# Two stacked layers of memory attention and a gated feed-forward, one core: the order of softmax and gate work, of the memory weighting in one-layer steps, and the form of the last output block are changed

## The chip, the cores and the metric

The kernel runs on one core of one Trainium2 chip. The metric is the device time of one execution in microseconds (us); the figure quoted for a kernel is the median of its runs. Five engines work side by side and meet through semaphores: TensorE (PE in the profile, with its weight loads as PEld), VectorE (DVE), ScalarE (ACT), GpSimd (POOL) and SyncE (SP). Matmul results go to PSUM, which this kernel uses as eight banks of 512 f32 values per partition.

## The reference

The input is 2048 tokens of 448 features. Two layers follow each other. Each is an attention with a memory that is handed from segment to segment, and then a feed-forward with a gate (ReGLU), both with a layer norm in front and a residual around:

```python
# attention: 64 segments of 32 tokens, 8 memory tokens, 16 heads of 256
for s in range(n_seg):
    h = jnp.concatenate([mem, x[:, s*32:(s+1)*32, :]], axis=1)       # 40 tokens
    q, k, v = (jnp.einsum('btd,dhe->bhte', h, W) for W in (Wq, Wk, Wv))
    scores = jnp.where(mask, jnp.einsum('bhqe,bhke->bhqk', q, k) * scale, -1e9)
    o = jnp.einsum('bhqk,bhke->bhqe', softmax(scores), v)
    o = jnp.einsum('bhte,hed->btd', o, Wo)
    mem = o[:, :8, :]                                                 # to the next segment
    outs.append(o[:, 8:, :])
# feed-forward, 448 -> 1792 -> 448
h = relu(x @ W_gate) * (x @ W_up);  y = h @ W_down
# whole
x = x + attention(layernorm(x)); x = x + feed(layernorm(x))          # twice, same weights
```

The memory of a segment comes out of the segment before, so the 64 segments of a layer run one after another.

## The kernel before, in words

**Weights.** Wq and Wk are folded into one matrix per head ahead of the loop (`A_sb`), Wv and Wo into another (`B_sb`). With these a step needs, for each half of the heads: `project` (hidden rows times `A_sb`, tiles `prj`, copied to `TQ` and `TZ`), `scores`, `softmax`, a transpose of the probabilities (`flipped`, tile `pps`, copied to `PT`), their product with the hidden rows `hk` (`weigh_m` and `weigh_x`, tiles `ya`, `yb`, `y1`, `y2`, copied to `Y`), and the product of `Y` with `B_sb` (`project_out` for features 0 to 383 in tile `ox`, `project_last` for the last 64 in `o3`).

**Steps.** `step` (line 695) handles one segment of each active layer. The second layer runs `LAG` = 4 segments behind the first, so steps g = 0 to 3 and 64 to 67 have one layer, g = 4 to 63 have two, and the hidden rows of both stand side by side in one matmul (80 columns, 40 in one-layer steps). `ms` are the layers whose memory goes on, `xs` those whose previous output is projected now. The heads fall into half 0 and half 1. Each half has a softmax of the memory queries (tile `Sm`, `m0` and `m1`, probabilities `PM`) and one of the segment's own queries (`Sx`, `x0` and `x1`, `PX`). `softmax` (line 651) gives four closures, called by index: [3] `lift`, [0] `first`, [1] `exp`, [2] `second`. With a mask (both layers active) `lift` adds it and `first` takes the maximum and subtracts it; without one `lift` does both and `first` nothing. `exp` is ACT's exponential on tile `se`, `second` sums, inverts and scales to `PM` or `PX`.

**Feed-forward.** Every odd step from g = 3 on carries one `Feed` (line 469): the feed-forward of 64 tokens of each layer. At g = 3 and 5, and in the last ones, only one layer has tokens, so it is 64 columns and not 128. `residual` adds the attention's output (collected with features on the partitions in `OT`, transposed on PE) to the tokens `x` and takes the layer-norm statistics (`row_stats`: batch-norm statistics and aggregate on DVE, `rstd` on POOL at lines 251 and 252); `norm` and `xposed` make `xT`. The 14 tiles of 128 gate and up columns go in units 0 to 3 of 4, 4, 4 and 2. `products(u)` puts a unit's up products in PSUM tile `ups` and its gate products in `gps`; for u = 3 both share one bank named `gps`. `gated(u)` copies `ups` to `ut` on ACT (the "up copy", a CAST) and then makes `hh` = max(`gps`, 0) * `ut` on DVE. `down` is the product with `Wd_sb` in `dps`; `down_out` adds the residual and stores.

**Order.** PE's order is that of the program text: `in_order` (line 80) ties every matmul to the one before. DVE and ACT are wrapped in `InOrder` (line 93), which does the same there, so all their instructions carry line 102; every matmul is line 144 (`mm`), every transpose line 152 (`tr`). A wait at the head of one of these queues therefore holds all behind it.

**PSUM banks.** `bank` (line 121) gives a new tile the one of the eight banks, among those not held, that by a running estimate comes free soonest: after a tile's last matmul the bank counts as free `after` ns later, a value given by name (700 if none). The tile's first matmul then waits for the last reader of whatever tile was in that bank before. For x1 of a feed step that value is 8000, for `gps` 1600, for `ups` 1000.

**The end.** At g = 67 (`end`) both x softmaxes are interleaved with the first products of the feed before; the outputs of half 0 and 1 go to `YB` column `XL`. Then a step g = 68 that only projects out (`if not chains`), and the lines from 1018 on: the residual, the rest of the feed before (`fed`), and the last feed (`ff`), whose output leaves by two stores on SP (line 569), beside a copy `xh` of the residual that came by DMA (line 489).

Of the kernel before, what the change touches and what calls it, by code (L numbers as in the profile page):

```python
# [9 lines left out]
F32 = mybir.dt.float32  # L10
I32 = mybir.dt.int32
AF = mybir.ActivationFunctionType
ALU = mybir.AluOpType
# [47 lines left out]
def build_kernel(ctx, tc, A_x, A_mem0, A_Wq, A_Wk, A_Wv, A_Wo, B_W_gate, B_W_up, B_W_down, out,  # L61
# [407 lines left out]
    class Feed:  # L469
# [10 lines left out]
        def residual(self):  # L480
            tp = bank([P, 4, 128], BF, "otp")
            for kd in range(4):
                tr(tp[:, kd, :], OT[:, kd, :], ident[:])
            dve.tensor_tensor(self.x[:], tp[:].rearrange("p k d -> p (k d)")[:, 0:DM], self.x[:], op=ALU.add)
            self.st = row_stats(self.x)
            if not self.first:
                self.xh = main.tile([P, DM // 2], BF, tag="xh", name="xh", bufs=2)
                for c in range(2):
                    nc.sync.dma_start(self.xh[64 * c:64 * c + 64, :], self.x[0:TB, HALF[c]])
# [70 lines left out]
        def down_out(self):  # L560
            i, dps = self.i, self.dps
            if self.first:
                dve.tensor_tensor(self.nx[TB:P, :], dps[TB:P, 0:DM], self.x[TB:P, :], op=ALU.add)
                self.st = row_stats(self.nx)
                nc.sync.dma_start(xa[(i + 2) % 3][0:TB, :], self.nx[TB:P, :])
            if self.second and not self.first:
                dve.tensor_tensor(self.xh[:], dps[:, 0:DM // 2], self.xh[:], op=ALU.add)
                for c in range(2):
                    nc.sync.dma_start(out_dram[block(i - LAG // BLK), HALF[c]], self.xh[64 * c:64 * c + 64, :])
            elif self.second:  # L570
                dve.tensor_tensor(self.x[0:TB, :], dps[0:TB, 0:DM], self.x[0:TB, :], op=ALU.add)
                nc.sync.dma_start(out_dram[block(i - LAG // BLK)], self.x[0:TB, :])
            if self.first and i + 3 < nblk:
                nc.sync.dma_start(self.x[TB:P, :], x_dram[block(i + 3)])
# [76 lines left out]
    def softmax(Sp, n, dst, keep, tag, mask=None):  # L651

        mx = main.tile([P, n], F32, tag=f"mx{tag}", name="mx")
        se = main.tile([P, n, L], F32, tag=f"se{tag}", name="se")
        ssum = main.tile([P, n], F32, tag=f"ssum{tag}", name="ssum")
        rs = main.tile([P, n], F32, tag=f"rs{tag}", name="rs")

        def lift():
            if mask is not None:
                dve.tensor_tensor(se[:], Sp[:], mask, op=ALU.add)  # L660
            else:
                shift(Sp)

        def first():
            if mask is not None:
                shift(se)

        def shift(src):
            dve.tensor_reduce(mx[:], src[:], axis=AX.X, op=ALU.max)
            dve.tensor_tensor(se[:], src[:], mx[:].unsqueeze(2).to_broadcast([P, n, L]), op=ALU.subtract)  # L670

        def exp():
            act.activation(se[:], se[:], AF.Exp, scale=SCALE)

        def second():
            dve.tensor_reduce(ssum[:], se[:], axis=AX.X, op=ALU.add)
            dve.reciprocal(rs[:], ssum[:])
            if keep is not None:
                dve.tensor_tensor(rs[:], rs[:], keep, op=ALU.mult)
            dve.tensor_tensor(dst[:, :, 0:L], se[:], rs[:].unsqueeze(2).to_broadcast([P, n, L]), op=ALU.mult)  # L680

        return first, exp, second, lift
# [12 lines left out]
    def step(g, ff, pre, late):  # L695
# [7 lines left out]
        if g == 0:  # L703
            lo = 0
        end = g == nsteps - 1
        if g == nsteps:
            lo, hi = XL, XO[1] + SEG
        ox = None

        def ox_open():  # L710
# [14 lines left out]
        def scores(hf, m, x):  # L725

            if not ms:
                m = False
            both = len(chains) == 2
            Sm = bank([P, 2, L], F32, "Sm", 1100) if m else None  # L730
            Sx = bank([P, 4, L], F32, "Sx", 2500 if hf == 0 else 3500 if ff is None else 8000) if x else None
            groups = [(half, c) for half in range(2) for c in chains]

            def mem(kds):
                for kd in kds:
                    mm(Sm[:, :, :], queries(hf, 2, kd), moving(hb, j, kd, (0, 1)),
                       start=(kd == KD[0]), stop=(kd == KD[-1]), skip_group_check=True)
# [12 lines left out]
            if m and x and not both:  # L750
                mem(KD)
                mask()
                own(KD)
            elif m and x:
                mem(KD[:3])
                own(KD[:3])
                mem(KD[3:])
                own(KD[3:])
            elif m:
                mem(KD)  # L760
            elif x:
# [19 lines left out]
        def weigh_x(hf, hk, PT, between=None):  # L781

            def keep(eng, c, t0, src):
                n = src.shape[-1] // SEG
                xo = XL if end else XO[c]
# [37 lines left out]
        def project_last():  # L823
# [21 lines left out]
            if g == nsteps:  # L845
                places = [(0, XO[1]), (SEG, XL)]
            else:
                places = [(o + (TB if c == 0 else 0), XO[c]) for c in xs]
            for to, x in places:
                dve.tensor_tensor(OT[r, 3, to:to + SEG], o3[r, x:x + SEG], os[r, x:x + SEG], op=ALU.add)  # L850

        def finish():
# [5 lines left out]
            if g == nsteps:  # L858
                dve.tensor_copy(OT[:, 0:3, 0:SEG], ox[:, :, XO[1]:XO[1] + SEG])
                dve.tensor_copy(OT[:, 0:3, SEG:TB], ox[:, :, XL:XL + SEG])  # L860
                return
            for c in xs:
                o2 = o + (TB if c == 0 else 0)
                dve.tensor_copy(OT[:, 0:3, o2:o2 + SEG], ox[:, :, XO[c]:XO[c] + SEG])
# [3 lines left out]
                for u in us:  # L868
                    ff.gate_up(u)

        if not chains:
            ox_open()
            project_out(0, 0, NT)
            project_last()
            project_out(1, 0, NT)
            finish()
            return None, None

        project(0, chains, hb, j, BANKS[0][0:2], pre)
        hk = hk_make()  # L880
# [9 lines left out]
        def memory_0():  # L890
            nonlocal m0
            m0, _ = scores(0, True, False)
            m0[3]()
            m0[1]()

        if late is not None:
# [14 lines left out]
            nonlocal pm  # L911
            pm = flipped(PM[0], 1, "m0") if ms else None

        project(1, chains, hb, j, BANKS[1][4:5], pre1, True, None, flip_m0)
        if ff is not None:
            ff.xposed_out()
        _, x0 = scores(0, False, True)
        weigh_m(0, hk, pm)
        m1, x1 = scores(1, True, True)
        m1[3]()  # L920
        m1[1]()
        x0[3]()
        if end:
            x1[3]()
            ff.open_rows((0, 1))
            x0[1]()
            x1[1]()
            x0[2]()
            ff.products(0)
            px0 = flipped(PX[0], 2, "x0", act)  # L930
            ff.gated(0)
            ff.products(1)
            x1[2]()
            px1 = flipped(PX[1], 2, "x1", act)
            ff.gated(1)
            weigh_x(0, hk, px0)
            weigh_x(1, hk, px1)
            return {}, None
        if ff is not None:
            x1[3]()  # L940
# [4 lines left out]
            x0[1]()  # L945
            m1[2]()
            x0[2]()
            x1[0]()
            x1[1]()
            feed(0)  # L950
            next_piece()
            ff.products(1)
            x1[2]()
            pm = flipped(PM[1], 1, "m1", act) if ms else None
            ff.gated(1)
            ff.products(2)
            px0 = flipped(PX[0], 2, "x0", act)
            weigh_m(1, hk, pm)
            ff.gated(2)
# [45 lines left out]

    dve.on = act.on = True
    pre, late = project_early(0, active(0), hTb[0], 0), None
    for g in range(nsteps + 1):
        if g == LAG - 1:
            set_mem(LAG, mem0T[:].unsqueeze(2), (1,))  # L1010
        i = (g - 3) // 2
# [4 lines left out]
            pre, late = step(g, None, pre, late)  # L1016

    ff = Feed(nblk + LAG // BLK - 1)
    fed.open_rows((2,))
    ff.residual()  # L1020
    for u in (2, 3):
        fed.products(u)
    for u in (2, 3):
        fed.gated(u)
    fed.down_part(0, 8)
    ff.norm()
    fed.down_part(8, FT)
    ff.xposed()
# [64 lines left out]
```

## Time and profile before

| | |
|---|---|
| median of 3 runs | 1599.95 us (1599.68 to 1600.59) |
| the profiled execution: its time | 1600.88 us |
| its span (first to last instruction) | 1599.0 us |
| mean granted TensorE clock | 0.999 |
| PE busy | 1574.0 us, 98% of the span, 41160 matmuls and transposes |
| PE weight loads busy | 1450.5 us, 91% |
| DVE busy | 1124.8 us, 70%, 3704 instructions |
| ACT busy | 744.1 us, 47%, 2088 instructions |
| POOL busy | 78.2 us, 5% |
| largest groups on PE | `prj` 541.7 us (15232 matmuls, 199 ns mean), `ox` 450.4 us (11424, 200 ns) |

How to read it: a matmul's recorded length (about 0.2 us) is much longer than the time between the starts of two (some 0.03 to 0.06 us), because matmuls are pipelined. The sum of lengths is counted once where they overlap, so "busy" says that some matmul was under way, not that PE ran at its best. A line of a timeline gives start, length, engine, line, operation, output and inputs with shapes, how many instructions were put together, and in brackets the idle time before it with what ended that. In a line of the chain that ended last, shares are of the span. A row of waits gives the engine, what waited, on what, then the sum of the waits in us, how often, and the mean.

### The profile page before, as it was taken

To read this page: it belongs to the slowest core of one execution; us is meant where nothing else is said; L and a number is where in the kernel's file an instruction comes from. 1 tells how busy PE (TensorE), PEld (TensorE's weight loads), DVE (VectorE), ACT (ScalarE), POOL (GpSimd) and SP (SyncE) were. 2 spreads that over 40 slices of the span, in tenths; PEclk is the share of its full clock that TensorE was granted. 3 is DMA by queue.
4 is the path that set the end of the run, shared out by engine and by line. 5 is a ranking of instruction groups with operands and counts; after the bars stand their busy time and mean duration, and the time that the engine had idled before them with its cause. 6 is when DMAs were issued, how large, how long until landed. Compare 5 with 4: busy or idle time off the path is not lost.

```text
span 1599.0 us, 89723 instructions
## 1 busy us (share of the span) xinstructions
PE 1574.0 (98%) x41160; PEld 1450.5 (91%) x41160; DVE 1124.8 (70%) x3704; ACT 744.1 (47%) x2088; POOL 78.2 (5%) x174
## 2 busy tenths in 40 slices
PE   9999999999999999999999999999999999999998
PEld 6688899999999999999999999999999999999897
DVE  7766677777667777776677777766777777667764
ACT  5644444454444444544444445444444454444443
POOL 3200000000000000000000000000000000000000
PEclk9999999999999999999999999999999999999999
DMA  8620000000000000000000000000000000000000
GB/s 235 211 73 9 8 9 9 5 8 9 9 9 9 10 9 7 7 10 9 9 9 9 9 6 7 9 9 9 9 9 9 8 6 9 9 8 7 6 7 9
DMA packets 28235, 33.24 MB, mean 21 GB/s; under 512 B 4168, under 2 KB 26960, under 8 KB 27856
## 3 DMA queue, kind: packets, MB, share of 16 engines
q1 hardware_dynamic: 26768, 23.82, 5.4%
q8 instruction: 322, 5.28, 1.4%
q0 software_dynamic: 1088, 3.68, 0.7%
q14 instruction: 57, 0.47, 0.1%
HBM read 23.70 MB, written 1.84 MB: 16 GB/s over the span
## 4 chain that ended last, share of the span: by engine, by line
PE 90%; DVE 7%; issue 1%; ACT 1%; SPq 0%; DMA 0%; POOL 0%; POOLq 0%; ACTq 0%
PE prj L144 31%; PE ox L144 24%; PE dps L144 5%; PE o L144 5%; PE y L144 4%; PE gps L144 4%; PE Sx L144 3%; PE ups L144 3%; DVE hh L102 3%; PE bps L144 1%; DVE se L102 1%; PE aps L144 1%; PE Sm L144 1%; PE pps L152 1%; PE tpw L152 1%
## 5 line engine op out<-in xcount | busy, mean ns | idle before, releaser
L144 PE MATMUL prj<-hT,A_sb 128*128 128x80 bf16 (+3 forms) x15232 | 541.7, 199 | 0.7 <-issue 0.5
L144 PEld LDWEIGHTS <-A_sb 128*128 128x128 bf16 (+1 forms) x15232 | 498.7, 99 | 23.5 <-issue 1.1
L144 PEld LDWEIGHTS <-B_sb 128*128 128x128 bf16 (+1 forms) x15232 | 497.5, 103 | 14.3 <-issue 0.6
L144 PE MATMUL ox<-Y,B_sb 128*128 128x80 bf16 (+3 forms) x11424 | 450.4, 200 | 0.6 <-issue 0.5
L102 ACT CAST TQ<-prj 128x480 bf16<-128x480 f32 (+1 forms) x380 | 184.5, 497 | 103.2 <-PE prj L144 96.5
L102 DVE CAST Y<-y 128x256 bf16<-128x256 f32 x376 | 151.3, 457 | 42.5 <-PE y L144 42.4
L102 ACT CAST Y<-y 128x512 bf16<-128x512 f32 (+2 forms) x392 | 137.1, 419 | 73.7 <-PE y L144 73.6
L102 ACT ACTIVATE se<-se 128x80 f32<-128x80 f32 (+1 forms) x270 | 81.9, 303 | 192.1 <-DVE se L102 187.8
L102 DVE CAST TQ<-prj 128x480 bf16<-128x480 f32 (+1 forms) x228 | 128.6, 573 | 6.8 <-PE prj L144 6.3
L144 PE MATMUL gps<-xT,Wg_sb 128*128 128x128 bf16 (+3 forms) x1904 | 128.5, 215 | 0.0
L144 PEld LDWEIGHTS <-Wu_sb 128*128 128x128 bf16 (+1 forms) x1904 | 106.8, 97 | 22.3 <-issue 13.0
L102 DVE SCALAR_TENSOR_TENSOR hh<-gps,ut 128x512 bf16<-128x512 f32 (+2 forms) x136 | 80.8, 595 | 50.7 <-ACT ut L102 33.3
L144 PEld LDWEIGHTS <-hk 40*128 40x128 bf16 (+1 forms) x1950 | 99.6, 96 | 13.5 <-issue 2.3
L102 ACT COPY os<-o 64x16 f32<-64x16 f32 (+3 forms) x135 | 25.8, 191 | 176.4 <-PE o L144 174.8
L144 PE MATMUL ups<-xT,Wu_sb 128*128 128x128 bf16 (+3 forms) x1632 | 106.7, 216 | 0.5 <-DVE xT L102 0.5
L144 PEld LDWEIGHTS <-Wg_sb 128*128 128x128 bf16 (+1 forms) x1904 | 106.7, 97 | 0.5 <-issue 0.5
L102 ACT CAST TZ<-prj 64x320 bf16<-64x320 f32 (+2 forms) x264 | 97.0, 378 | 17.2 <-DVE TZ L102 13.6
L144 PE MATMUL dps<-Wd_sb,hh 128*128 128x448 bf16 (+1 forms) x504 | 93.1, 342 | 0.0
L102 ACT COPY PT<-pps 128x256 bf16<-128x256 bf16 (+1 forms) x136 | 47.3, 347 | 97.4 <-PE pps L152 97.4
L144 PE MATMUL y<-PT,hk 40*128 40x256 bf16 (+1 forms) x1280 | 91.2, 248 | 0.9 <-ACT Y L102 0.8
L102 DVE TENSOR_REDUCE ssum<-se 128x2 f32<-128x80 f32 (+1 forms) x270 | 73.3, 272 | 24.2 <-ACT se L102 24.2
L144 PEld LDWEIGHTS <-TQ 128*128 128x128 bf16 x1938 | 86.7, 97 | 1.7 <-issue 1.3
(121 smaller groups left out, 1898.5 us busy)
## 6 DMA issues: line engine op xcount, KB each, us to landing
wo<-in_A_Wo_dram POOLq DMA_DIRECT2D x8, 448.0 KB, 4.9
nat<-in_A_Wq_dram SPq DMA_DIRECT2D x8, 384.0 KB, 5.0
nat<-in_A_Wk_dram SPq DMA_DIRECT2D x8, 384.0 KB, 5.1
nat<-in_A_Wv_dram SPq DMA_DIRECT2D x8, 384.0 KB, 4.9
xa<-in_A_x_dram SPq DMA_DIRECT2D x32, 56.0 KB, 2.2
xa<-xp SPq DMA_DIRECT2D x32, 56.0 KB, 1.9
xp<-in_A_x_dram SPq DMA_DIRECT2D x30, 56.0 KB, 2.7
out_dram<-xa SPq DMA_DIRECT2D x30, 56.0 KB, 2.5
```

The costliest lines, as they stand in the source:

```text
L102: r = f(*a, **k)
L144: in_order(nc.tensor.matmul(out, lhsT, rhs, **k))
L152: in_order(nc.tensor.transpose(out, src, idn))
```

## The change

Five things are edited.

1. `softmax`: without a mask, `lift` now takes only the maximum, and the subtraction moves into `first`. So calls of `m0[0]()`, `m1[0]()` and, at the end, `x0[0]()` and `x1[0]()` are added.
2. In the steps with a feed, x1's `first` stands behind the up copy and `hh` of unit 0, and x1's exponential behind the up copy and `hh` of unit 1; the transpose of half 1's `PM` comes ahead of, and x1's `second` behind, the products of unit 2. x1's bank counts as free after 1600 ns in place of 8000 when both layers are active.
3. In one-layer steps the transpose of half 0's `PM` stands ahead of the last bank of half 1's projection, and `weigh_m(0)` ahead of x0's scores. In two-layer steps both stay where they were.
4. At g = 67 both x softmaxes run together, and the products of unit 3 come up between the two transposes of `PX`; the weighting of half 0 goes ahead of `gated(1)`, and `gated(3)` follows that of half 1.
5. Step g = 68 is gone. The last output block is projected with the 64 tokens as the stationary side and the 448 features moving: 56 matmuls of 64x448, even `t` to partitions 0 to 63 of one bank, odd `t` to partitions 64 to 127 of another. It is added to `x` without a transpose: ACT copies the odd part to SBUF and DVE adds twice (`residual_of`). Eight down products of the feed before follow the projection, then that feed's unit 2. The two last stores are issued from SP and ACT.

```diff
@@ Feed
+        def residual_of(self, ot):
+            odd = main.tile([P, DM], F32, tag="odd", name="odd")
+            act.copy(odd[0:TB, :], ot[1][TB:P, 0:DM])
+            both = main.tile([P, DM], F32, tag="both", name="both")
+            dve.tensor_tensor(both[0:TB, :], ot[0][0:TB, 0:DM], self.x[0:TB, :], op=ALU.add)
+            dve.tensor_tensor(self.x[0:TB, :], both[0:TB, :], odd[0:TB, :], op=ALU.add)
+            self.statistics()
...
-                for c in range(2):
-                    nc.sync.dma_start(out_dram[block(i - LAG // BLK), HALF[c]], self.xh[64 * c:64 * c + 64, :])
+                for c, eng in enumerate((nc.sync, nc.scalar)):
+                    eng.dma_start(out_dram[block(i - LAG // BLK), HALF[c]], self.xh[64 * c:64 * c + 64, :])
@@ softmax
             else:
-                shift(Sp)
+                peak(Sp)
         def first():
+            src = Sp
             if mask is not None:
-                shift(se)
+                peak(se)
+                src = se
+            dve.tensor_tensor(se[:], src[:], mx[:].unsqueeze(2).to_broadcast([P, n, L]), op=ALU.subtract)
@@ scores
-            Sx = bank([P, 4, L], F32, "Sx", 2500 if hf == 0 else 3500 if ff is None else 8000) if x else None
+            Sx = bank([P, 4, L], F32, "Sx", 2500 if hf == 0 else 3500 if ff is None else 1600 if both else 8000) if x else None
@@ step
-        project(1, chains, hb, j, BANKS[1][4:5], pre1, True, None, flip_m0)
+        if len(chains) == 1:
+            flip_m0()
+            project(1, chains, hb, j, BANKS[1][4:5], pre1, True)
+        else:
+            project(1, chains, hb, j, BANKS[1][4:5], pre1, True, None, flip_m0)
...
+        if len(chains) == 1:
+            weigh_m(0, hk, pm)
         _, x0 = scores(0, False, True)
-        weigh_m(0, hk, pm)
+        if len(chains) == 2:
+            weigh_m(0, hk, pm)
         m1, x1 = scores(1, True, True)
...
         if end:
+            x0[0]()
+            x0[1]()
             x1[3]()
+            x1[0]()
+            x1[1]()
             ff.open_rows((0, 1))
-            x0[1]()
-            x1[1]()
             x0[2]()
+            x1[2]()
             ff.products(0)
+            ff.products(1)
             px0 = flipped(PX[0], 2, "x0", act)
             ff.gated(0)
-            ff.products(1)
-            x1[2]()
+            ff.products(3)
             px1 = flipped(PX[1], 2, "x1", act)
+            weigh_x(0, hk, px0)
             ff.gated(1)
-            weigh_x(0, hk, px0)
             weigh_x(1, hk, px1)
+            ff.gated(3)
...
             x0[2]()
-            x1[0]()
-            x1[1]()
             feed(0)
             next_piece()
+            x1[0]()
             ff.products(1)
+            ff.gated(1)
+            x1[1]()
+            pm = flipped(PM[1], 1, "m1", act) if ms else None
+            ff.products(2)
             x1[2]()
-            pm = flipped(PM[1], 1, "m1", act) if ms else None
-            ff.gated(1)
-            ff.products(2)
             px0 = flipped(PX[0], 2, "x0", act)
@@ after the loop
     ff = Feed(nblk + LAG // BLK - 1)
+    ot = [bank([P, 512], F32, "ot") for _ in range(2)]
+    for hf in range(2):
+        for t in range(NT):
+            r = slice(64 * (t % 2), 64 * (t % 2) + 64)
+            mm(ot[t % 2][r, 0:DM], YB[hf][:, t, XL:W], B_sb[:, hf, t, :], start=(hf == 0 and t < 2),
+               stop=(hf == 1 and t >= NT - 2), tile_position=(0, r.start), skip_group_check=True)
+    fed.down_part(0, 8)
+    ff.residual_of(ot)
     fed.open_rows((2,))
-    ff.residual()
-    for u in (2, 3):
-        fed.products(u)
-    for u in (2, 3):
-        fed.gated(u)
-    fed.down_part(0, 8)
+    fed.products(2)
+    fed.gated(2)
     ff.norm()
```

More of the change, by code (lines that the diff above doesn't have):

```diff
@@ L484, in residual, with statistics @@
             dve.tensor_tensor(self.x[:], tp[:].rearrange("p k d -> p (k d)")[:, 0:DM], self.x[:], op=ALU.add)
+            self.statistics()
[5 more added lines that the diff above has]
+            dve.tensor_tensor(self.x[0:TB, :], both[0:TB, :], odd[0:TB, :], op=ALU.add)
+            self.statistics()
+        def statistics(self):
             self.st = row_stats(self.x)
@@ L661, in lift, with peak @@
             else:
-                shift(Sp)
+                peak(Sp)
         def first():
+            src = Sp
             if mask is not None:
-                shift(se)
-        def shift(src):
+                peak(se)
+                src = se
+            dve.tensor_tensor(se[:], src[:], mx[:].unsqueeze(2).to_broadcast([P, n, L]), op=ALU.subtract)
+        def peak(src):
             dve.tensor_reduce(mx[:], src[:], axis=AX.X, op=ALU.max)
-            dve.tensor_tensor(se[:], src[:], mx[:].unsqueeze(2).to_broadcast([P, n, L]), op=ALU.subtract)
         def exp():
@@ L705, in step @@
         end = g == nsteps - 1
-        if g == nsteps:
-            lo, hi = XL, XO[1] + SEG
         ox = None
@@ L784, in keep @@
                 n = src.shape[-1] // SEG
-                xo = XL if end else XO[c]
+                xo = XL if g == nsteps - 2 else XO[c]
                 dst = YB[hf][:, t0:t0 + n, xo:xo + SEG]
@@ L844, in project_last @@
             o = (g - 1) % BLK * SEG
[L845 to L849, printed above, removed]
+            for to, x in [(o + (TB if c == 0 else 0), XO[c]) for c in xs]:
                 dve.tensor_tensor(OT[r, 3, to:to + SEG], o3[r, x:x + SEG], os[r, x:x + SEG], op=ALU.add)
@@ L857, in finish @@
             o = (g - 1) % BLK * SEG
[L858 to L861, printed above, removed]
             for c in xs:
@@ L869, in feed @@
                     ff.gate_up(u)
[L871 to L877, printed above, removed]
         project(0, chains, hb, j, BANKS[0][0:2], pre)
@@ L893, in memory_0 @@
             m0[3]()
+            m0[0]()
             m0[1]()
@@ L912, in flip_m0 @@
             pm = flipped(PM[0], 1, "m0") if ms else None
-        project(1, chains, hb, j, BANKS[1][4:5], pre1, True, None, flip_m0)
+        if len(chains) == 1:
[3 more added lines that the diff above has]
+            project(1, chains, hb, j, BANKS[1][4:5], pre1, True, None, flip_m0)
         if ff is not None:
             ff.xposed_out()
+        if len(chains) == 1:
+            weigh_m(0, hk, pm)
         _, x0 = scores(0, False, True)
-        weigh_m(0, hk, pm)
+        if len(chains) == 2:
+            weigh_m(0, hk, pm)
         m1, x1 = scores(1, True, True)
         m1[3]()
+        m1[0]()
         m1[1]()
@@ L1007, in build_kernel @@
     pre, late = project_early(0, active(0), hTb[0], 0), None
-    for g in range(nsteps + 1):
+    for g in range(nsteps):
         if g == LAG - 1:
```

## The prediction

> **What bounds the kernel now.** I read the page's busy times and clock, then the waits of PE, then the timeline of one period of the two-layer steps, then the same places in the one-layer steps and the tail.
>
> ```profile
> PE 1574.0 (98%) x41160; PEld 1450.5 (91%) x41160; DVE 1124.8 (70%) x3704; ACT 744.1 (47%) x2088; POOL 78.2 (5%) x174
> PEclk9999999999999999999999999999999999999999
> PE 90%; DVE 7%; issue 1%; ACT 1%; SPq 0%; DMA 0%; POOL 0%; POOLq 0%; ACTq 0%
> ```
>
> TensorE is busy nearly throughout, at its full granted clock, and carries 90% of the chain that ended last. So an edit pays where PE waits, or where it issues less.
>
> ```profile
> PE gps L144 <- DVE hh L102: 6.7, 29, 0.2
> PE pps L152 <- DVE PX L102: 2.1, 3, 1.3
> PE pps L152 <- ACT ut L102: 1.7, 2, 1.4
> PE gps L144 <- ACT ut L102: 1.5, 2, 0.8
> ```
>
> The first row is one wait in each of 29 equal steps. How it arises is in the timeline of one of them (start, length):
>
> ```profile
> 811.16 0.33 DVE L102 TENSOR_TENSOR se<-se,mx 128x160 f32<-128x160 f32 x1
> 811.58 0.34 ACT L102 ACTIVATE se<-se 128x160 f32<-128x160 f32 x1 [1.88 <-DVE se L102]
> 811.59 0.83 PE L144 MATMUL gps<-xT,Wg_sb 128*128 128x128 bf16 x12
> 811.83 0.57 ACT L102 CAST ut<-ups 128x512 bf16<-128x512 f32 x1
> 812.45 0.22 PE L152 MATMUL pps<-ident,PM 128*128 128x128 bf16 x1
> ...
> 813.83 0.68 DVE L102 SCALAR_TENSOR_TENSOR hh<-gps,ut 128x512 bf16<-128x512 f32 x1
> ...
> 814.06 0.28 PE L144 MATMUL yb<-PT,hk 128*128 128x128 bf16 x3
> ...
> 814.57 0.49 PE L144 MATMUL gps<-xT,Wu_sb 128*128 128x128 bf16 x6 [0.23 <-DVE hh L102]
> ```
>
> ACT stands idle 1.88 us before half 1's exponential at 811.58; the first up copy, whose products ended at 810.5, is queued behind it. Stall A: a run of 12 matmuls takes 0.67 (810.25, 810.92, 811.59), so the transpose of PM was due at 812.26 and came at 812.45, because its PSUM bank was read by that copy: 0.18. Stall B: the three yb matmuls take 0.11, so gps was due at 814.17 and came at 814.57, because its bank was read by the second hh: 0.40. I count from start to start: matmuls overlap in the pipeline, so PE shows as busy in most of a stall. The step with half as many tokens in the feed-forward (g=5) has the same two waits, larger:
>
> ```profile
> 173.46 0.34 ACT L102 ACTIVATE se<-se 128x160 f32<-128x160 f32 x1 [1.87 <-DVE se L102]
> 174.11 0.22 PE L152 MATMUL pps<-ident,PM 128*128 128x128 bf16 x1 [1.40 <-ACT ut L102]
> 176.24 0.39 PE L144 MATMUL gps<-xT,Wu_sb 128*128 128x64 bf16 x8 [0.79 <-ACT ut L102]
> ```
>
> In the tail PE waits for the softmaxes, projects, and waits through a chain of small steps:
>
> ```profile
> 1573.48 0.28 PE L152 MATMUL pps<-ident,PX 128*128 128x128 bf16 x2 [0.43 <-DVE PX L102]
> 1575.81 0.28 PE L152 MATMUL pps<-ident,PX 128*128 128x128 bf16 x2 [1.35 <-DVE PX L102]
> 1582.47 2.62 PE L144 MATMUL ox<-Y,B_sb 128*128 128x64 bf16 x84
> 1587.13 0.18 DVE L102 BATCH_NORM_AGGREGATE mv<-stats 128x2 f32<-128x6 f32 x1
> 1594.84 1.11 SPq L569 DMA_DIRECT2D out_dram<-xh  x2
> ```
>
> **The change, part by part.** The program built from the new kernel has the same PE order in the two-layer steps; only DVE, ACT and the PSUM banks differ there.
>
> *Up copies first (29 steps, g=7 to 63).* ACT now runs ut0, ut1, the exponential, PT of PM; DVE runs hh0, then half 1's maximum and subtraction, then hh1. With x1's bank declared free after 1600, gps of unit 2 takes x1's bank, the transpose of PM takes x0's (read long before, at 808.46), and gps of unit 3 takes the bank of that transpose. Laid out with the durations of the trace: ut0 from 810.45 (products ready) to 811.02; hh0, which also waits for gps0 (ready 811.09), 811.12 to 811.81; maximum and subtraction to 812.40; ut1 811.79 to 812.36; exponential 812.49 to 812.83; PT 812.74 to 813.00. PE: PM's transpose at 812.26 without a wait, unit 2 to 813.66, two transposes, then ya at 813.77, which needs PT (813.00: margin 0.77), yb, and gps of unit 3 at 814.00, which needs PT too. hh1 ends at 813.15, half 1's PX at 813.95, ut2 at 815.10, hh2 at 815.82; the down products start at 815.75 and reach unit 2 at 817.26 (eight of 0.19 later). So nothing new waits. Each step saves 0.18 + 0.40, less 0.01 for rounding: 0.57; 29 of them 16.6. From below, gps behind yb may need 0.08 as it does at 1541, not 0.03, which makes 0.52 (15.1); from above 0.58 (16.8).
>
> *The same at g=5.* The products are half as long, so ya would be due at 173.41, while PT, behind ut1 and the exponential (173.79 to 174.13), ends at 174.31: ya waits 0.95. Then yb, and gps of unit 3 at 174.56, not 176.24: 1.7 saved. If PT came as late as ut0 does now, 1.0; without ya's wait about 2.2.
>
> *At g=3* (one layer, 64 tokens; half 1's subtraction now stands behind hh0). hh0 is late at 131.94 because DVE works through eight semaphore waits before it, one each 0.1. I put it at 131.5, the subtraction to 132.2, the exponential to 132.6, PT to 132.8, ut2 to 133.9, and gps of unit 3 at 133.9 where it stands at 133.37: 0.5 lost (from 0.2 gained, if the waits run beside other work, to 1.0 lost). At g=65 all of it is covered: no change.
>
> *Memory weighting sooner.* Seven one-layer steps (g=0 to 3, 64 to 66). PM's transpose moves 12 matmuls (0.30) ahead and ya, yb come before x0's scores. In a step without a feed PE now waits 0.15 for the copies of ya and yb before ox (1557.43 to 1557.60); they come 0.24 sooner and that wait goes, but PM of half 1, which PE awaits 0.10, comes only 0.09 sooner: 0.1 each, five times. In the two with a feed PM ends as PE gets there now, so the transpose gains nothing, and the scores no longer cover the 0.5 to PT: 0.2 lost each. Together 0.1 gained (from 0.8 lost to 0.9 gained).
>
> *Tail.* Both softmaxes end by 1574.22 (now 1575.75). PE: unit 1 ends at 1573.58, transposes, unit 3's products (0.47, moved here from 1586.5) to 1574.26, half 1's transposes at 1574.75 (their bank waits for ut0). Then a new wait: y2 of half 0 takes unit 1's up bank, and ut1 stands on ACT behind PT and a Y copy, until 1576.28; hh1 stands on DVE behind y2's copies, until 1577.70, and the second bank of the new projection is the one it reads. So the projection starts at 1577.75 (now 1577.38). It is 28 pairs of 448 columns; the nearest rows are the 14 pairs of 224 columns at 1592.85, one each 0.096 (1.53 less one length, 0.28, over 13), so 0.19 for 448 and 5.3 in all; four such matmuls at 51.02 give 0.21, 6.0 in all. It ends at 1583.29 with the last one's length. Then the add from PSUM, 0.63 (a row of that shape), beside ACT's copy (0.53); the second add, between 0.39 (bf16) and 0.63, taken as 0.63 for its fp32 operands; statistics 0.63. The aggregate starts at 1585.3, 1.8 sooner than 1587.13, and the rest hangs on it by the same steps; hh2 before it on DVE costs nothing, as xn waits 1.2 for POOL. 0.05 goes to a bank that waits for xh. The two last stores are issued by SP and ACT side by side: of 1.11 one half, 0.56. Tail 2.3 (1.0 to 3.0).
>
> [...]
>
> Sum: 16.6 + 1.7 - 0.5 + 0.1 + 2.3 = 20.2. The profiled execution took 1600.88 (span 1599.0), so it would take 1580.7; it stands 0.93 above the median 1599.95, from which I forecast 1579.7. The ends add to 15.3 and 23.1: 1576.9 to 1584.7.
>
> **Rivals.**
> 1. *PT late, slower.* If PT of PM, now behind the exponential, ends over 0.77 later than laid out, ya waits in all 29 steps. At g=5's 0.95 this takes 27.6 back: 1607. For: g=5 and g=3 do so on paper. Against: the margin, and DVE has nothing else there.
> 2. *Only idle time is saved.* PE's shown idle time is 0.25 per step (0.23 and 0.02), 7.3 in all, and 3.6 from the rest: 1589. Against: matmuls of 0.22 start 0.056 apart, so busy time hides waits. [...]
> 3. *The banks do not come free sooner.* Other tiles get the freed banks and gps of unit 3 still waits; only 3.6 is left: 1596.3. Against: the built program's waits name PT there.
> [...]
>
> **How the numbers follow.** Forecast 80%, rival 1 5%, rival 2 5%, rival 3 5%, rival 4 3%, no change 2%. Faster than by 0.2% (what a measurement here can tell): 93%; within 2%; slower 5%. The range runs from 1575.5 to 1587: the forecast's own, a little wider for steps I did not see, and rival 4; 0.8.
>
> **What would show it.** In the changed profile, PE's wait for hh (29 times) is gone, gps of unit 3 follows yb at 0.03, two feed steps in a row are 45.05 apart where they are 45.62, the projection runs 5.3, the aggregate comes 1.8 sooner relative to the last scores. I am wrong if ya waits for PT in every period, or if waits of PE for another copy appear in the even steps.

## The result and the profile after

The changed kernel takes 1582.06 us (median of 4 runs, 1580.68 to 1583.94) where the kernel before takes 1600.27 beside it: a ratio of 0.9884, 95% interval 0.9867 to 0.9901, some 18 us less. The forecast was 1579.7 in a range of 1575.5 to 1587. The profiled execution has a span of 1581.0 (before: 1599.0). Its page shows the engines and the chain of work that ended last as follows; its row of the granted clock is all nines, as before.

```profile
PE 1563.5 (99%) x40988; PEld 1443.7 (91%) x40988; DVE 1126.1 (71%) x3701; ACT 745.4 (47%) x2088; POOL 78.0 (5%) x174
PE 97%; DVE 1%; issue 0%; ACT 0%; DMA 0%; SPq 0%; POOL 0%; POOLq 0%; ACTq 0%
```

PE's busy time fell by only 10.5, although the span fell by 18.0: the share of PE in the chain rose from 90% to 97% and DVE's fell from 7% to 1%. The waits of PE in the trace after (what waited, on what, sum, how often, and last the longest single wait, which is not the mean that it was called above):

```profile
PE ya L144 <- ACT PT L102: 1.7, 2, 1.0
...
PE gps L144 <- ACT ut L102: 0.7, 1, 0.7
```

The wait of `gps` for `hh`, 29 times, is gone. What is left are single waits: `ya` for `PT` at g=3 and g=5, `gps` for `ut` at g=3, which was there before as well, and those of the last step. The timeline of one period after (start, length):

```profile
801.95 0.58 ACT L102 CAST ut<-ups 128x512 bf16<-128x512 f32 x1 [0.75 <-PE ups L144]
...
803.29 0.58 ACT L102 CAST ut<-ups 128x512 bf16<-128x512 f32 x1 [0.76 <-PE ups L144]
...
803.76 0.22 PE L152 MATMUL pps<-ident,PM 128*128 128x128 bf16 x1
...
804.06 0.34 ACT L102 ACTIVATE se<-se 128x160 f32<-128x160 f32 x1 [0.18 <-DVE se L102]
804.31 0.25 ACT L102 COPY PT<-pps 128x128 bf16<-128x128 bf16 x1
...
805.27 0.28 PE L144 MATMUL ya<-PT,hk 128*128 128x128 bf16 x2
...
805.50 0.61 PE L144 MATMUL gps<-xT,Wu_sb 128*128 128x128 bf16 x8
```

PE goes from one to the next without a wait: the transpose of PM follows the products by 0.06 and `gps` of unit 3 follows the last `yb` by 0.03. `PT` ends at 804.56, 0.71 ahead of `ya`. Shifted by 8.50, every one of these times is within 0.1 of the prediction's layout.

To see where the time went I cut each trace at the first transposes (`kps`) of certain steps. All figures are us; the rows below "after" are the experiments of the next section, and the last column gives the length of a stretch of half clock in the end, which comes up there.

| kernel | g 0-3 | g 3-5 | g 5-7 | g 7-63 | g 63-67 | end from g=67 | span | half clock at the end |
|---|---|---|---|---|---|---|---|---|
| before | 44.33 | 39.93 | 44.98 | 1277.93 | 81.61 | 33.26 | 1599.0 | 3.42 |
| after | 44.54 | 40.55 | 43.29 | 1261.64 | 82.17 | 32.02 | 1581.0 | 3.42 |
| bank only | 45.37 | 39.90 | 43.50 | 1261.78 | 80.89 | 34.48 | 1582.7 | 6.84 |
| order only | 45.65 | 40.35 | 44.13 | 1261.78 | 81.30 | 33.23 | 1583.5 | 3.42 |
| both of these | 44.90 | 40.34 | 43.29 | 1261.78 | 81.58 | 34.39 | 1582.9 | 6.82 |
| end only | 46.01 | 40.21 | 44.97 | 1277.50 | 82.46 | 32.20 | 1600.4 | 3.40 |
| after, again | 44.24 | 40.58 | 43.30 | 1261.88 | 81.37 | 32.32 | 1580.6 | 3.42 |
| extra transposes | 44.83 | 42.42 | 43.30 | 1261.99 | 80.68 | 31.04 | 1581.3 | none (3.42 at g=0 and at g=3) |
| end's banks | 43.43 | 40.69 | 43.30 | 1261.97 | 80.68 | 28.75 | 1575.7 | none |
| best | 44.80 | 39.94 | 43.51 | 1261.97 | 80.74 | 28.74 | 1576.5 | none |
| one ACT copy | 44.68 | 40.49 | 43.82 | 1262.27 | 81.30 | 30.39 | 1579.8 | none |
| two ACT copies | 42.92 | 40.50 | 46.12 | 1276.75 | 81.71 | 30.50 | 1595.6 | none (3.41 at g=5) |

Between before and after, the 28 periods from g=7 to g=63 give 16.29 (two feed steps in a row are 45.05 apart, before 45.62; 0.27 of it is one longer wait that the trace before has at 1223.0). The step g=5 gives 1.69, g=3 takes 0.62, the end gives 1.24. What is left takes 0.6, although the twenty-ninth period's gain of 0.57 lies in it. The sum is 18.0.

### The profile page after: what moved, and what is told of

Read it like the earlier page. It is cut to its first block, busy times and chain, and to the rows that moved or that the text cites. A ratio compares the mean times of both kernels' runs of the same rounds, so it can differ in the third digit from the quotient of the medians.

```text
span 1581.0 us, 89369 instructions
## 1 busy us (share of the span) xinstructions
PE 1563.5 (99%) x40988; PEld 1443.7 (91%) x40988; DVE 1126.1 (71%) x3701; ACT 745.4 (47%) x2088; POOL 78.0 (5%) x174
## 4 chain that ended last, share of the span: by engine, by line
PE 97%; DVE 1%; issue 0%; ACT 0%; DMA 0%; SPq 0%; POOL 0%; POOLq 0%; ACTq 0%
PE prj L144 31%; PE ox L144 25%; PE gps L144 6%; PE ups L144 6%; PE dps L144 5%; PE o L144 5%; PE y L144 4%; PE Sx L144 3%; PE pps L152 2%; PE bps L144 1%; PE aps L144 1%; PE Sm L144 1%; PE tpw L152 1%; PE ya L144 1%; PE yb L144 1%; PE kps L152 1%
## 5 line engine op out<-in xcount | busy, mean ns | idle before, releaser
L144 PEld LDWEIGHTS <-B_sb 128*128 128x128 bf16 (+1 forms) x15008 | 489.6, 103 | 14.3 <-issue 1.2
L144 PE MATMUL ox<-Y,B_sb 128*128 128x80 bf16 (+2 forms) x11256 | 443.6, 200 | 0.9 <-issue 0.8
```

The costliest lines, as they stand in the source:

```text
L144: in_order(nc.tensor.matmul(out, lhsT, rhs, **k))
```

## The experiments

### The bank alone, and the order alone

The change in the feed steps has two parts, and the prediction reckoned with both together. The first run keeps the old order and changes only the number after which x1's bank counts as free.

```diff
-            Sx = bank([P, 4, L], F32, "Sx", 2500 if hf == 0 else 3500 if ff is None else 8000) if x else None
+            Sx = bank([P, 4, L], F32, "Sx", 2500 if hf == 0 else 3500 if ff is None else 1600 if both else 8000) if x else None
```

> The kernel before with one number changed: x1's bank counts as free after 1600 and not 8000 in two-layer steps with a feed. The up copies stay behind half 1's exponential, and the end and the one-layer steps are as before. Theory 1 (the banks made both stalls): the transpose of PM and the products of unit 3 get banks that were read long ago, so both waits go although ACT and DVE work in the old order; 29 steps of 0.57, that is 16.6 less than before, two feed steps in a row 45.05 apart. Theory 2 (the order made them: a bank's reader is late because the up copies are late): the freed bank only hands the wait to another tile, at most stall A of 0.18 goes, 5 less, steps 45.4 apart or more. Theory 3 (both parts are needed): nothing within 0.2%, 45.6 apart.

Measured: 1583.3 against 1602.08 for before, ratio 0.9889 (0.9874 to 0.9903), two feed steps 45.05 apart. That is the whole gain of the change, from one number. The timeline of a period of this kernel:

```profile
803.55 0.34 ACT L102 ACTIVATE se<-se 128x160 f32<-128x160 f32 x1 [1.87 <-DVE se L102]
...
803.79 0.57 ACT L102 CAST ut<-ups 128x512 bf16<-128x512 f32 x1
804.24 0.22 PE L152 MATMUL pps<-ident,PM 128*128 128x128 bf16 x1
...
805.80 0.68 DVE L102 SCALAR_TENSOR_TENSOR hh<-gps,ut 128x512 bf16<-128x512 f32 x1
...
805.97 0.61 PE L144 MATMUL gps<-xT,Wu_sb 128*128 128x128 bf16 x8
```

ACT still stands idle 1.87 ahead of half 1's exponential, and the first up copy still runs late, until 804.36. But the transpose of PM starts at 804.24, during that copy: it has another bank and no longer waits for it. In the same way `gps` of unit 3, which here has the bank of that transpose and no longer the one of unit 1's `gps`, starts at 805.97 while the second `hh` is still reading, until 806.48. So ACT's idle time is no cost in itself; what cost was that PE needed the very banks that the late `ut` and `hh` were reading.

The second run has the new order and the old bank time. (The split of `lift` and `first` and its added calls belong to it and are left out here.)

```diff
...
-            x1[0]()
-            x1[1]()
             feed(0)
             next_piece()
+            x1[0]()
             ff.products(1)
+            ff.gated(1)
+            x1[1]()
+            pm = flipped(PM[1], 1, "m1", act) if ms else None
+            ff.products(2)
             x1[2]()
-            pm = flipped(PM[1], 1, "m1", act) if ms else None
-            ff.gated(1)
-            ff.products(2)
...
```

> The kernel before with the new order of the feed steps (up copies and hh of units 0 and 1 ahead of half 1's exponential, lift split) and x1's bank still counted as free after 8000. Theory 1 (the banks): the transpose of PM still waits for the first up copy and unit 3's products for the second hh, so the waits stay in name; at most 0.2 a step is saved, 6 in all. Theory 2 (the order): the same banks, but their readers are done sooner (first up copy 1.2 before the transpose of PM is due, second hh 0.8 before unit 3 is due), so both stalls go: 45.05 per two steps, 16.6 less, and about 1.2 more from the steps g=5 (1.7 gained) and g=3 (0.5 lost). If both this run and the one with the bank alone give 16 or more, either part is enough and they do not add up. Theory 3 (both parts are needed): 45.6 apart, nothing.

Measured: 1585.01 against 1602.08, ratio 0.9895 (0.9881 to 0.991), 45.05 apart as well. Its timeline:

```profile
804.03 0.58 ACT L102 CAST ut<-ups 128x512 bf16<-128x512 f32 x1 [0.75 <-PE ups L144]
...
805.84 0.22 PE L152 MATMUL pps<-ident,PM 128*128 128x128 bf16 x1
...
806.11 0.69 DVE L102 SCALAR_TENSOR_TENSOR hh<-gps,ut 128x512 bf16<-128x512 f32 x1
...
807.57 0.61 PE L144 MATMUL gps<-xT,Wu_sb 128*128 128x128 bf16 x8
```

Here every tile has the bank that it has in the kernel before, as banks are given in the order of the matmuls, which is the same. But the readers are early: the first up copy ends 1.23 before the transpose of PM, the second `hh` ends 0.77 before `gps` of unit 3. So each part removes both stalls by itself, and together they remove them once. Where they differ is at the two steps with 64 tokens: at g=5 the bank alone gives 1.48 (44.98 to 43.50), the order alone 0.85, both 1.69; at g=3 the order takes 0.4 and the bank nothing.

Both parts in the feed steps, with the end and the one-layer steps as before (the two diffs above together):

> New order and new bank time together in the feed steps, with the one-layer memory weighting and the end as before. By the prediction's terms 16.6 + 1.7 - 0.5 = 17.8 less than before. The whole change measured 18.2 less, so if the rest of it (memory weighting and end) is worth the 2.4 that the prediction gave, this should be at 15.8 less; if the end gave only what the trace after shows (about 1.2) and the one-layer steps lost about as much, this is at 18.

Measured: 1582.79 against 1602.08, ratio 0.9886 (0.9872 to 0.9901). The whole change gave 0.9884. So the rest of the change, memory weighting and end, can't be told from nothing here, and the table shows one reason: what the end could give is of the size of one stretch of half clock, and these vary (6.82 in this trace).

### The end

The new end alone, without the edits in the feed steps and the one-layer steps:

```diff
...
             ff.products(0)
+            ff.products(1)
             px0 = flipped(PX[0], 2, "x0", act)
             ff.gated(0)
-            ff.products(1)
-            x1[2]()
+            ff.products(3)
...
+    ot = [bank([P, 512], F32, "ot") for _ in range(2)]
...
+    ff.residual_of(ot)
...
```

> Only the new end: last softmaxes together, last block with tokens on the partitions, last stores from two queues; feed steps and one-layer steps as before. The prediction's term is 2.3 less. The trace after says 1.24 less between the last step's first transposes and the end, with the projection at a granted clock of 0.50 for its first 3.2 us. If the slow clock belongs to this end (PE waits of 2.1 us just ahead of it), it shows here again and the saving is 1.2; if it depended on chance, the projection runs all 28 pairs at 0.19 in 5.3 and the saving is 2.7 to 2.9.

Measured: 1600.58 against 1602.08, ratio 0.9992 (0.9983 to 1.0002), and 32.20 for the end: 1.1 less than before. The slow clock shows here again. The timeline of the end of the changed kernel says what precedes it:

```profile
1557.81 0.27 PE L152 MATMUL pps<-ident,PX 128*128 128x128 bf16 x2 [0.32 <-ACT ut L102]
...
1559.36 0.82 PE L144 MATMUL y<-PT,hk 40*128 40x256 bf16 x8 [0.96 <-ACT ut L102]
...
1560.78 6.97 PE L144 MATMUL ot<-B_sb,Y 128*64 128x448 bf16 x55 [0.30 <-DVE hh L102]
...
1569.66 0.18 DVE L102 BATCH_NORM_AGGREGATE mv<-stats 128x2 f32<-128x6 f32 x1
...
1577.43 0.51 ACTq L580 DMA_DIRECT2D out_dram<-xh  x1
```

Three waits on banks, then the projection (the first of its 56 matmuls stands ahead of the third wait). The view by windows gives, for a stretch, its length, the busy time and number of instructions of each engine, the granted clock, and the DMA share and rate. In the trace after, the first and the second half of the projection:

```profile
1560.80:1563.90 3.10, 3.10 (x18) 1.96 (x19) 0.29 (x1) 0.40 (x3) 0.00 (x0) 0.50 0.02 5
1564.00:1567.20 3.20, 3.20 (x36) 2.32 (x34) 0.00 (x0) 0.00 (x0) 0.00 (x0) 1.00 0.00 0
```

At a granted clock of 0.50 a pair of 448 columns takes 0.374, at 1.00 it takes 0.189. The trace before has the same at the same place:

```profile
1577.40:1581.00 3.60, 3.60 (x72) 3.60 (x72) 0.42 (x2) 0.86 (x3) 0.00 (x0) 0.53 0.02 5
```

The page's row of the clock, in 40 slices, hides this: 3.4 us of half clock are less than a tenth of a slice of 40 us.

To see how far this belongs to chance, the changed kernel was run a second time, with no edit.

> The changed kernel a second time, for the part of its time that varies. If the slow clock ahead of the last block belongs to the kernel's own waits, the projection's first half again shows half the rate (0.37 a pair). If the 3.4 us stretches of slow clock lie by chance against the program, their start relative to the last step moves by some us against the 11.3 us after that step's first transposes seen before, and the end is between 30.5 (no slow stretch) and 33.5 long (two) where it was 32.0. Steps g=0 to 2 and 64 to 66 vary by up to 1 each through waits that the trace gives to issue alone.

Measured: 1582.93 against 1601.9, ratio 0.9887 (0.9872 to 0.9902); half clock from 1560.86 to 1564.28, the end 32.32. In finer windows the half clock lasts 3.40 to 3.42 in seven traces (twice in one of them), and 6.82 and 6.84 (two such stretches in a row) in two. In the clock records of the traces before and after it begins 1573.544 and 1556.478 after the first record of full clock, 461 and 456 times 3.4133, and the full clock behind it lasts 17.067, five times 3.413. Its start moves against the program: in the trace after it begins 11.5 after the first transposes of g=67, in this second run of the same kernel 12.5. In the 3.41 ahead of the drop PE was busy for 57% in the trace before and for 62% in the trace after, by the profile. The kernels with one and two extra ACT copies, shown below, have the changed kernel's end line for line, but no half clock in it:

```profile
1560.00:1566.00 6.00, 5.70 (x61) 4.07 (x60) 1.25 (x4) 1.20 (x4) 0.00 (x0) 1.00 0.01 3
```

Their ends are 30.39 and 30.50 long, against 32.02 and 32.32 with one stretch: a stretch costs 1.5 to 1.9. In the 3.41 ahead of the drop of the trace after the longest gap of PE was 0.96 (1558.4 to 1559.36), and the clock fell all the same.

Does the clock follow from PE's idle time, or from the waits' cause? In the next run the waits stay as they are and PE transposes the identity into an unread part of a bank meanwhile; the output is not touched.

```diff
...
+        def junk(k):
+            for i in range(k):
+                tr(made["x1"][:, 2 + i % 6, :], ident[:], ident[:])
...
-            weigh_x(0, hk, px0)
+            weigh_x(0, hk, px0, lambda: junk(13))
             ff.gated(1)
             weigh_x(1, hk, px1)
+            junk(7)
...
```

> The changed kernel with 20 extra transposes of the identity on PE that nothing reads, 13 where PE waits for the second up copy and 7 where it waits for the second hh in the last step, so that PE works through waits that stay as long as they are. If the slow clock follows from PE's idle time in the stretch before it, the granted clock stays at 1.00, the projection runs 28 pairs at 0.19 in 5.3 where it took 6.6, and the end is 1.3 to 1.6 shorter, although PE does more. If the clock has nothing to do with that idle time, the end is as long as before or up to 0.3 longer.

Measured: 1582.95 against 1601.9, ratio 0.9888 (0.9872 to 0.9905), so no difference to the changed kernel in the whole time; the parts say more. The first row is the projection, the second a stretch in step g=3:

```profile
1562.50:1567.50 5.00, 5.00 (x54) 3.72 (x55) 0.29 (x1) 0.37 (x3) 0.00 (x0) 1.00 0.01 3
135.30:138.60 3.30, 3.30 (x31) 1.67 (x27) 0.29 (x1) 0.26 (x1) 0.00 (x0) 0.52 0.00 0
```

The projection ran at full clock and took 5.3 as forecast there, the end 31.04, 1.0 to 1.3 less. In this execution the half clock fell on g=0 and on g=3 instead; at g=3, where PE waits 1.0 and 0.7 close together, it cost 1.9 (42.42 against 40.55). One execution can't prove that the extra transposes held the clock up, since the same end without them also stayed up in two others.

PE's busy share by itself does not tell when the clock falls. Each of these two rows is a window of 3.41: the first, of this run, stands just ahead of the drop at g=0, with PE busy for 67%; the second, of the changed kernel's second run at g=3, begins 419 times 3.4133 ahead of that run's drop at 1560.86, has 51% and was followed by full clock.

```profile
84.26:87.68 3.42, 2.28 (x88) 1.98 (x86) 2.36 (x10) 0.60 (x3) 0.00 (x0) 1.00 0.28 82
130.68:134.10 3.42, 1.75 (x50) 1.53 (x46) 2.41 (x9) 1.71 (x6) 0.00 (x0) 1.00 0.02 7
```

What PE streamed divides the windows better in the two traces before and after. Cut each into windows of 3.4133 from its first record of full clock, and count for each matmul that starts in a window its moving columns, times the share of 128*128 that its active rows and columns make up. The window ahead of the drop at the last block holds 1664 such columns in the trace before and 1696 in the trace after; of the other windows at full clock in which a matmul starts none holds fewer than 3536 and 3840. This was read off the traces; no run was made to test it.

The next run takes the waits away by giving the tiles of the last step other banks (`like` takes the bank of an earlier tile).

```diff
...
-            px1 = flipped(PX[1], 2, "x1", act)
-            weigh_x(0, hk, px0)
+            px1 = flipped(PX[1], 2, "x1", act, made["Sx", 0])
+            weigh_x(0, hk, px0, None, (made["Sx", 1], made["x0"]))
             ff.gated(1)
-            weigh_x(1, hk, px1)
+            weigh_x(1, hk, px1, None, (ff.ps[0][0], made["x1"]))
...
-    ot = [bank([P, 512], F32, "ot") for _ in range(2)]
+    ot = [bank([P, 512], F32, "ot", like=t) for t in (fed.ps[0][1], made["y1", 0])]
...
```

> The changed kernel with the PSUM banks of the last step's tiles chosen by hand: the transpose of half 1's PX takes half 0's score bank, and the weighting and the last block take banks whose readers are early. PE's waits for the first up copy (0.3), the second up copy (1.0) and the second hh (0.5) ahead of the last block go; the copies of Y, 0.6 after the weighting, are then next. If banks alone cause these waits, the projection starts about 1.5 sooner. If the clock then also stays up, as there is less idle time, another 1.3 to 1.6, together 3. If ACT's order of the copies is what is late, nothing.

Measured: 1578.25 against 1601.9, ratio 0.9859 (0.9845 to 0.9874); the changed kernel's second run on the same chip took 1582.93. The end is 28.75, 3.3 to 3.6 less, as expected. Its timeline (its lines stand one lower, so matmuls are line 145):

```profile
1555.43 0.29 PE L153 MATMUL pps<-ident,PX 128*128 128x128 bf16 x2
...
1555.65 1.18 PE L145 MATMUL y<-PT,hk 40*128 40x256 bf16 x10
...
1556.76 5.49 PE L145 MATMUL ot<-B_sb,Y 128*64 128x448 bf16 x56
```

From the transpose of half 1's PX to the projection it is 1.3; in the changed kernel it was 3.0 to the second matmul of the projection. And the clock stays up throughout it:

```profile
1556.80:1562.00 5.20, 5.20 (x57) 3.15 (x58) 0.83 (x3) 1.25 (x5) 0.00 (x0) 1.00 0.01 3
```

The mean granted clock, which is on record for every run, says that this is no single case: it is 1.000 in all four runs here, and 0.998 or 0.999 in all eight of the changed kernel (one stretch of half clock takes 0.001 off the mean). Chance keeps a part, since both runs with one ACT copy, shown below, have the changed kernel's end and 1.000 too.

### A version of the parts that paid

The next run keeps the old order in the feed steps with the new bank time, the new end with the banks above, and the earlier memory weighting only in one-layer steps without a feed.

```diff
...
-        if len(chains) == 1:
+        if len(chains) == 1 and ff is None:
             flip_m0()
             project(1, chains, hb, j, BANKS[1][4:5], pre1, True)
...
```

> Of the change only what the runs and traces showed to pay: the kernel before with x1's bank at 1600 (the old order of exponential and up copies, no loss at g=3), memory weighting sooner only in one-layer steps without a feed, the new end with the banks of the run before. Expected from the parts: 16.6 for the 29 steps, 1.5 at g=5, 1.2 for the end, 3 for its banks and clock: 22 less than before, that is 3 to 4 less than the changed kernel. If the order is needed for the even steps after all, or the end's banks give nothing, 18 to 19.

Measured: 1578.16 against 1601.9, ratio 0.9861 (0.9846 to 0.9875): 23.7 less than before by the medians, 4.8 less than the changed kernel's second run on the same chip, and no different from the run before it. Step g=3 is back at 39.94, g=5 costs 0.2 more (43.51): the order of the up copies, by which the change is named, is worth nothing in the sum once the bank comes free sooner.

### How much slack PT has

The slower rival of the prediction was that `PT` of PM, put behind the exponential, comes late in each step. Extra copies on ACT ahead of it, which nothing reads, measure the slack.

```diff
             x1[1]()
+            if len(chains) == 2:
+                for _ in range(2):        # or range(1)
+                    act.copy(scrap[:], still[:])
             pm = flipped(PM[1], 1, "m1", act) if ms else None
```

> The changed kernel with one copy of 128x512 on ACT that nothing reads, put between half 1's exponential and the copy PT of PM in every two-layer step with a feed. In the trace after, PT ends at 804.56 and ya, which needs it, starts at 805.27: 0.71 of slack. A copy of about 0.5 to 0.6 ends inside that slack, so if the margin is read rightly the 28 periods from g=7 to g=63 take the same 1261.8 (within 0.5), and only g=5, where ya waits for PT already, loses about 0.5. If PT is on the path in the even steps too (rival 1), each period loses 0.5: 14 more.

> The same with two such copies, 1.0 to 1.2 in all. Past the slack of 0.71, so ya waits for PT in each period by about 0.4 to 0.5: 28 periods lose 11 to 14 against the changed kernel and g=5 about 1. If the work after the first copy has slack that the trace does not show, less.

Measured: with one copy (0.604) the 28 periods take 1262.27, 0.3 to 0.6 more in all, and g=5 loses 0.5; the time is 1581.14 against 1601.0 (0.987, 0.9835 to 0.9905). With two (1.26) they take 1276.75, 15 more or 0.53 each, slightly above the forecast, and the time is 1597.69 (0.9978, 0.9966 to 0.9989): most of the gain is lost. At g=5 it is 2.8 and not about 1: PE's wait of 1.9 there was followed by a stretch of half clock from 175.7 to 179.1. The timeline of a period with two copies, and then its row of waits:

```profile
812.33 1.26 ACT L102 CAST scrap<-still 128x512 f32<-128x512 bf16 x2
...
813.80 0.27 PE L144 MATMUL ya<-PT,hk 128*128 128x128 bf16 x2 [0.35 <-ACT PT L102]
```

```profile
PE ya L144 <- ACT PT L102: 13.5, 31, 1.9
```

So the slack of 0.71 is real and it is all there is: 0.60 fits, and of 1.26 some 0.53 comes through.

## Why the prediction was right, and where not

**Up copies first, 16.6.** Right in size: 45.05 apart, 0.57 a period. The two stalls were where it put them, and the layout held to 0.1. (29 of 0.57 make 16.5, not 16.6.) It took order and bank as one edit, though, and laid the gain to both; the runs showed that either alone is enough. As the text put it, "gps of unit 3 takes the bank of that transpose": in the run with the bank alone, that ended stall B.

**g=5, 1.7 gained, and g=3, 0.5 lost.** Measured 1.69, and 0.41 with the order (40.34 against 39.93). At g=5 `ya` waits 0.75 for `PT`, where the layout had 0.95.

**Memory weighting, 0.1.** Of the 0.2 lost in each of the two steps with a feed, the one at g=3 is seen: the five kernels with both edits (one row with a slow stretch there left out) stand 0.15 to 0.35 above the one with the feed parts alone, and in the trace after PE stands idle 0.13 there for PM. The one at g=65 is not: that step takes 23.10 in four of the six kernels with both edits, 23.36 and 23.41 in the others, and 23.18 with the feed parts alone. Of the steps without a feed g=64 shows the gain: 16.12 in all seven kernels that have the edit there, 16.28 in all five that don't, so 0.16 where the forecast had 0.1. In the others it can't be read: steps 0 to 3 together vary from 42.92 to 46.01 over the kernels, through waits of up to 1.1 that the trace puts down to issue alone, and their cause stays open. The 1.1 that the steps behind g=63 seem to lose in the trace after may be of this kind, as a second run of the same kernel had 0.8 less there.

**Tail, 2.3.** This term was mis-sized: 1.24 and 0.94 in the two traces. The step that failed is the time of the projection, "so 0.19 for 448 and 5.3 in all". The start was good to 0.2 (11.79 after the first transposes, laid out as 11.98), the pair takes 0.189 as taken from the rows, and the last stores are 0.6 shorter as said. But 5.3 is a time at full clock, and the clock was at 0.50 for 3.42, so it took 6.6. The trace before already showed such a stretch in the old block:

```profile
1577.38 4.15 PE L144 MATMUL ox<-Y,B_sb 128*128 128x64 bf16 x84
```

The next 84 of `ox` took 2.62 there, a row that the prediction quotes. From that row (0.029 from one `ox` to the next, 168 of them) and from the 56 of `o`, 1.07 in all (0.032 a pair, 28 pairs), I estimate 5.8 for the old block at full clock; it took 7.6. So the layout set a new block at full clock against an old end with a stretch of half clock in it, and the 1.8 by which the aggregate was to come sooner held what that stretch had cost. The aggregate came 0.7 sooner (20.67 after the first transposes of g=67, before 21.36). Whether the new block takes 5.3 or 6.6 or more goes with the new wait for banks ahead of it, which the prediction saw, and with where the clock's stretches happen to fall.

**Rivals.** PT late: refuted, slack 0.71. Only idle time saved (1589): refuted by 45.05. (From 812 to 815 of the trace before, around the stalls, PE shows as busy for 92%, 2.75 of 3.00; the 0.25 of idle time shown is less than half of the 0.58 lost.) Banks not free sooner (1596.3): refuted. Rival 4, to which the lower end of the range goes back, was a faster projection: no run shows a rate above that of its rows. The rows gave 0.19 for a pair, and it took 0.189 at full clock; the new block's 5.3, in the run with the extra transposes, stands against the 5.8 estimated for the old one at equal clock.

The sum of 20.2 stands against 18.0 in the profiles and 18.2 in the medians; the end accounts for 1.1 of the difference and the varying one-layer steps for about as much.

## What to carry to other kernels

When PE waits for a reader that is late, ask which of two things to change: the reader's place in its queue, or the bank it holds; where the allocation goes by estimates, one number may do what a reordering does, with fewer side effects. Read the granted clock over stretches of a few us wherever PE waits several times in a row, since half a clock for 3.4 us can cost as much as the waits themselves and a row of 40 slices doesn't show it. Take away the waits ahead of a dense block first: here they cost 1.7, and the clock behind them 1.5 to 1.9 more.

## What had not been expected of the hardware

The granted clock fell to 0.50 for some 3.41 us although PE did not stand still for more than 1.9 at a time in the 3.41 us ahead, and was busy for 44% to 67% of it by the profile. Other stretches with 51% (the changed kernel's second run, from 130.68) and 61% (the trace after, from 130.28) were not followed by a drop, so the busy share does not decide it; the columns streamed divide the windows of the traces before and after better, but that was not tested. The same end of the program ran with none or one such stretch, and the old end with one or two. This alone moves the time of one kernel by 1.5 to 1.9, more than the new end was measured to give.
